# A list scheduler that ranks by what follows, six plans instead of one, and ScalarE as the engine that rounds the second batch's queries and keys

## The chip, the cores and the metric

The kernel runs as one program on one core of a Trainium2 chip. The core has five engines that each take their own instructions strictly in order: TensorE (PE: matrix products; PEld is its loading of weights), VectorE (DVE), ScalarE (ACT), GpSimd (POOL) and SyncE (SP, which here only issues transfers; 16 DMA engines carry them out). The metric is the device time of one execution in microseconds.

## The reference

Three layers follow each other, on 2 batches of 768 tokens.

- Attention, 8 heads of 64 columns. Six sign bits of `q @ proj` and `k @ proj` make a bucket number for each query and key; `mask = q_bucket == k_bucket`; `scores = where(mask, q @ k.T / 8, -1e9)`; `attn = softmax(scores)`; `out = attn @ v`.
- On the heads put side by side (768 x 512): `u = x + real(fft(fft(x, axis=1), axis=2))`, a normalisation of `u`'s rows, and `u + relu(un @ w_ch1) @ w_ch2` with an inner width of 2048.
- `h = gelu(x @ w_in)`, split into `u` and `v` of 512 columns; `v` is normalised and scaled by `g_ln`, mixed over the tokens by `w_sg` plus a bias, and `x + (u * v_s) @ w_out` is the result.

The weights come in 64-bit floats; all is held to float32 accuracy, so nearly every product is made of a high and a low half in 16 bits.

## The kernel before, in words

**Attention.** A head has six tiles of 128 queries, so there are 96 tiles, 48 in each batch. For a tile TensorE makes the scores `s` (L394), VectorE takes the row maximum (L404), ScalarE the exponential `e` (L406). Then `e` is cut into two 16-bit halves `eh` (L251 on ScalarE or L253 on GpSimd, and the remainder L258 on GpSimd), SyncE turns `eh` over by a transposing transfer (L445), and TensorE multiplies by the values (18 products per tile, L462 to L464). In batch 0 two tiles of six (`FLIP`) are turned over on TensorE instead (L430, L457, L460).

**Queries and keys.** Before its scores a head is prepared in `stacks`: `q1`, a rounded copy of the head's queries and keys (entry `hi` of `ENG`: VectorE L255 in batch 0, GpSimd L253 in batch 1, called by `copy`), `k2`, the rest (VectorE L265), and four moves of 64 partitions to the other half (`mv`; S stands for a transfer by SyncE, A for ScalarE, P for GpSimd; `ENG0` is for the very first head). Then ScalarE writes the one-hot bucket codes into `q1` and `k1` (L287, L289), out of a product `ct` (L360) of the sign bits (`bits`, L280, from `z`, L311). Heads whose number is in `FULL` skip this: their scores are one product in full float32 rather than two rounded ones.

**Weights.** A weight arrives as pieces `wide` of 64-bit words (L221); VectorE makes 32-bit floats of each in three steps (L226 to L228), ScalarE sums their squares (L230), one small product adds the sums over the partitions (`pb`, L139), and the two halves are written by ScalarE (L239) and VectorE (L241). `w1a` is made during batch 0's attention, the other halves of the two big weights (`w2a`, `w1b`, `w2b`) during batch 1's, the last layer's weights after it.

**Stages.** Attention of batch 0; then, at the same time, attention of batch 1, the Fourier step of batch 0 (`fft`; products y L549 and p L575) with its normalisation, and the first of the big layers for batch 0 (`ch`: c1 L667, its outputs halved by L675 and L676, and c2 L688); then the Fourier step and `ch` of batch 1; then the last layer (gi L764, sg L787, go L804).

**What sets the order.** The program is first recorded in one order. The class `Order` then plans anew: it takes every operation with a cost for each engine, walks through time, and on each engine starts the operation that is ready and stands first in the recorded order. Its transfer costs are guesses of the kernel's own. The plan's order is then fixed on each engine (`apply`): an engine whose next instruction waits stands still, even if a later one could run.

Of the kernel before, what the change touches and what calls it, by code (L numbers as in the profile page):

```python
# [21 lines left out]
P = 128  # L22
# [32 lines left out]
WB = (3, 2)  # L55
ENG = ({'oh': 'A', 'hi': 'D', 'mv': 'SSSS', 'cast': 'PPA', 'sub': 'P'}, {'oh': 'A', 'hi': 'P', 'mv': 'SSSS', 'cast': 'AAP', 'sub': 'P'})
GP = ''
FULL = (3, 11)
ZP = (False, False)
CP = (False, False)  # L60
ENG0 = {'hi': 'D', 'mv': 'AASA', 'oh': 'A'}
W_ATT0 = 1.5
# [868 lines left out]
class Node:  # L931
    def __init__(self, k, eng):
        self.k, self.eng = k, eng
        self.ins, self.acc, self.dep, self.succ, self.tiles = [], [], {}, [], []
        self.cost, self.size, self.turn, self.port = 0.0, 0, False, False


class Order:
# [5 lines left out]
    GAP = {"DVE": 0.19, "POOL": 0.13}  # L944
    LOOK, OVER = 12, 0.3
    LAP = {"PE": 0.0, "DVE": 0.075, "ACT": 0.1, "POOL": 0.045, "SP": 0.0}

# [34 lines left out]
    def cost(self, i, rd, wr):  # L982
# [32 lines left out]
    def read(self):  # L1015
# [3 lines left out]
        for i in self.tc.nc.cur_bb.bb.instructions:  # L1019
# [14 lines left out]
            n.cost += self.cost(i, rd, wr)  # L1034
            n.port = self.port(i, e, rd, wr)
            if e == "SP":
                n.turn = "Transpose" in type(i).__name__
                n.size = wr[0][2] * wr[0][5] * wr[0][7] if not wr[0][1] else (wr[0][2] - wr[0][1]) * wr[0][5] * wr[0][7]
# [52 lines left out]
    def choose(self, nodes, now, t, held):  # L1091
        n = nodes[heapq.heappop(now)]
        wait = held - t - 0.2
        if n.port and wait > 0.0 and now:
            for k in sorted(now)[:self.LOOK]:
                m = nodes[k]
                if not m.port and m.cost < wait + self.OVER:
                    now.remove(k)
                    heapq.heapify(now)
                    heapq.heappush(now, n.k)  # L1100
                    return m
        return n

    def plan(self):
# [10 lines left out]
        need = [len(n.dep) for n in nodes]  # L1115
        when, start = [0.0] * N, [0.0] * N
# [4 lines left out]
        wire, held = 0.0, [0.0, 0.0]  # L1121

        def room(n):
# [25 lines left out]
        for _ in range(N):  # L1149
            while True:  # L1150
                best = None
                for e in clock:
                    while later[e] and later[e][0][0] <= clock[e]:
                        heapq.heappush(now[e], heapq.heappop(later[e])[1])
# [5 lines left out]
                while later[e] and later[e][0][0] <= t:  # L1160
                    heapq.heappush(now[e], heapq.heappop(later[e])[1])
                n = self.choose(nodes, now[e], t, held[e == "DVE"] if e in ("DVE", "POOL") else 0.0)
                r = room(n)
                if r is None:
                    continue
                if r > t:
                    heapq.heappush(later[e], (r, n.k))
                    continue
                break
# [17 lines left out]
            start[n.k] = t  # L1187
            done = end + self.AFTER[e]
            for p in {self.home[x] for x in n.tiles}:
# [12 lines left out]
            for m in n.succ:  # L1202
# [6 lines left out]
                if not need[m.k]:  # L1209
                    push(m)  # L1210
        return order
# [100 lines left out]
```

## Time and profile before

| what | us |
|---|---|
| median of 3 runs | 706.52 |
| lowest and highest of them | 701.41, 707.3 |
| profiled execution, own time | 704.52 |
| its span, first to last instruction | 702.7 |

The profile is of one execution. The span is 1.8 us shorter than the execution's own time. A share says how much of the span an engine was busy; a wait is put down to the instruction that ended it; the granted clock is TensorE's, as a part of 2.4 GHz.

### The profile page before, as it was taken

The page shows a single profiled execution, that of the slowest core. Times are in us where ns is not written, and L with a number is a line of the kernel's source. Part 1 is how long each engine was busy: PE and PEld are TensorE (multiplying, and loading weights), DVE is VectorE, ACT ScalarE, POOL GpSimd, SP SyncE. Part 2 cuts the span into 40 slices and gives each one's busy share as a digit, 9 for nine tenths or more (in the row PEclk, how much of TensorE's full clock was granted, in tenths as well). Part 3 has the DMA queues.
Part 4 walks back from the last instruction along what each step waited for, and adds up shares of the span by engine and source line. Part 5 has one row for each costly group of instructions (what it writes and reads, how often), then busy time and mean ns, then how long its engine had stood idle before and what let it go on. Part 6 is the DMA issues. An engine that isn't in the chain of part 4 may idle for free.

```text
span 702.7 us, 12575 instructions
## 1 busy us (share of the span) xinstructions
PE 634.3 (90%) x4832; PEld 415.7 (59%) x4832; DVE 500.3 (71%) x1136; ACT 343.8 (49%) x533; POOL 237.0 (34%) x203
## 2 busy tenths in 40 slices
PE   3689998976787889899999999988999999999997
PEld 0577777844464666668687658645767444444443
DVE  6777756659799879798667299668663367776663
ACT  4778888965475765466562224214552044222010
POOL 1355656668367953255454032000000012111000
PEclk8799999987798999999999999999999999999999
DMA  8699999999998997869654014853100022112234
GB/s 324 180 173 164 187 231 187 207 231 278 226 198 177 202 206 197 181 149 216 131 93 137 1 31 76 255 138 102 61 1 1 1 46 45 25 24 40 64 90 120
DMA packets 184044, 94.79 MB, mean 135 GB/s; under 512 B 166512, under 2 KB 167280, under 8 KB 183472
## 3 DMA queue, kind: packets, MB, share of 16 engines
q1 hardware_dynamic: 183408, 93.85, 60.1%
q8 instruction: 38, 0.62, 0.4%
q10 hardware_dynamic: 576, 0.14, 0.1%
q14 instruction: 22, 0.18, 0.1%
HBM read 39.50 MB, written 3.15 MB: 61 GB/s over the span
## 4 chain that ended last, share of the span: by engine, by line
PE 58%; DVE 12%; DMA 12%; issue 6%; ACT 5%; POOL 5%; SPq 1%; ACTq 0%; POOLq 0%; DVEq 0%
PE c L688 13%; PE c L667 11%; PE gi L764 9%; PE sg L787 7%; DMA et<-eh 5%; PE go L804 4%; PE s L394 4%; POOL eh L258 3%; PE z L311 3%; DMA wide<-w 2%; DMA wide<-w_in 2%; DVE nm L404 2%; DVE w L228 2%; ACT e L406 1%; PE po L457 1%
## 5 line engine op out<-in xcount | busy, mean ns | idle before, releaser
L258 POOL TENSOR_TENSOR eh<-e,eh 128x768 f16<-128x768 f32 x80 | 141.0, 1765 | 95.3 <-ACT eh L251 90.7
L667 PE MATMUL c<-unT,w 128*128 128x256 f16 x1152 | 136.9, 279 | 7.9 <-DVE h L676 6.0
L667 PEld LDWEIGHTS <-w 128*128 128x128 f16 x1152 | 114.3, 100 | 28.2 <-issue 8.6
L688 PE MATMUL c<-w,h 128*128 128x512 f16 x576 | 130.2, 381 | 0.0
L394 PE MATMUL s<-k,q 128*128 128x384 f32 x384 | 101.3, 392 | 22.8 <-ACT k L289 15.7
L404 DVE TENSOR_REDUCE nm<-s 128x1 f32<-128x768 f32 x96 | 91.0, 951 | 36.4 <-PE s L394 36.2
L406 ACT ACTIVATE e<-s,nm 128x768 f32<-128x768 f32 x96 | 85.5, 896 | 41.8 <-DVE nm L404 26.5
L688 PEld LDWEIGHTS <-h 128*128 128x128 f16 x576 | 55.8, 99 | 63.6 <-issue 2.4
L394 PEld LDWEIGHTS s<-k,q 128*128 128x128 f32 x384 | 68.2, 201 | 31.2 <-ACT k L289 16.3
L780 POOL TENSOR_TENSOR vh<-gv,vh 128x512 f16<-128x512 f32 x12 | 13.9, 1157 | 197.3 <-ACT vh L779 197.3
L462 PE MATMUL pav<-V,et 128*128 128x65 f16 x480 | 54.7, 198 | 16.7 <-DMA et<-eh 12.1
L462 PEld LDWEIGHTS <-et 128*128 128x128 f16 x480 | 45.4, 101 | 28.6 <-DMA et<-eh 16.2
L463 PE MATMUL pav<-V,et 128*128 128x64 f16 x480 | 54.3, 196 | 0.0
L464 PE MATMUL pav<-V,et 128*128 128x65 f16 x480 | 54.1, 198 | 0.0
L675 ACT ACTIVATE h<-c 128x256 f16<-128x256 f32 x96 | 35.2, 378 | 34.6 <-PE c L667 34.3
L764 PE MATMUL gi<-in,xT 128*128 128x512 f16 x216 | 50.5, 379 | 0.0
L676 DVE SCALAR_TENSOR_TENSOR h<-c,h 128x256 f16<-128x256 f32 x96 | 38.3, 415 | 16.8 <-ACT h L675 16.8
L764 PEld LDWEIGHTS <-xT 128*128 128x128 f16 x288 | 28.2, 98 | 35.0 <-issue 1.1
L463 PEld LDWEIGHTS <-et 128*128 128x128 f16 x480 | 45.9, 100 | 2.3 <-issue 1.6
L464 PEld LDWEIGHTS <-et 128*128 128x128 f16 x480 | 46.0, 100 | 0.0
L251 ACT ACTIVATE eh<-e 128x768 f16<-128x768 f32 x48 | 40.2, 840 | 7.2 <-DMA et<-eh 6.6
L253 POOL TENSOR_SCALAR eh<-e 128x768 f16<-128x768 f32 x32 | 30.6, 956 | 34.3 <-ACT e L406 28.2
(221 smaller groups left out, 999.7 us busy)
## 6 DMA issues: line engine op xcount, KB each, us to landing
wide<-w SPq DMA_DIRECT2D x24, 512.0 KB, 4.5
x<-qk SPq DMA_DIRECT2D x16, 384.0 KB, 4.5
k<-q SPq DMA_DIRECT2D x26, 192.0 KB, 3.6
wide<-w SPq DMA_DIRECT2D x4, 1024.0 KB, 8.8
wide<-w_in SPq DMA_DIRECT2D x16, 256.0 KB, 3.1
vst<-v SPq DMA_DIRECT2D x8, 396.0 KB, 4.2
y<-ot SPq DMA_DIRECT2D x12, 256.0 KB, 2.3
q<-k SPq DMA_DIRECT2D x14, 192.0 KB, 3.7
```

What stands on the lines that cost most here:

```text
L251: self.nc.scalar.activation(out, src, AF.Copy, scale=scale)
L258: (self.nc.vector if eng == "D" else self.nc.gpsimd).tensor_tensor(out=out, in0=a, in1=b, op=ALU.subtract)
L394: nc.tensor.matmul(s[:, hf, 0:HS], q[:, qs], k[:, hf * HS:(hf + 1) * HS], start=n == 0, stop=n == len(pairs) - 1)
L404: nc.vector.tensor_reduce(nm, x["s"], axis=AX.XY, op=ALU.max, negate=True)
L406: nc.scalar.activation(e.rearrange("p (a c) -> p a c", a=2), x["s"], AF.Exp, bias=nm)
L462: nc.tensor.matmul(pv[:, qt, 0:65], et[:, kb, :], V[:, hl, kb, 64:129], start=kb == 0, stop=False)
L463: nc.tensor.matmul(pv[:, qt, 0:64], et[:, kb, :], V[:, hl, kb, 0:64], start=False, stop=False)
L464: nc.tensor.matmul(pv[:, qt, 0:65], et[:, NT + kb, :], V[:, hl, kb, 64:129], start=False, stop=kb == NT - 1)
L667: nc.tensor.matmul(ps[:, 0:step], w1[kc][:, a, fo], uT[:, 4 * u + kc, o * P:o * P + step], start=m == 0, stop=m == 11)
L688: nc.tensor.matmul(ps, hs[n, half, f][:, a, j * P:(j + 1) * P], wv[:, w, :], start=f + m == 0, stop=f == NF - 1 and m == 2)
L764: nc.tensor.matmul(ps, xT[:, 4 * a + kc, :], w_in[kc][:, w, half * DM:(half + 1) * DM], start=n == 0, stop=n == 11)
L787: nc.tensor.matmul(ps, w_sg[kt][:, w, t * P:(t + 1) * P], vh[b][:, kt, a, :], start=n == 0, stop=n == 17)
```

## The change

Three entries of the tables at the top change. In batch 1 the rounding of queries and keys (`hi`) moves from GpSimd to ScalarE. Head 11 leaves `FULL` and is prepared as the other heads are. Of the first head's four moves, the two that write `q2` go to GpSimd (they were one on ScalarE, one on SyncE), and the last, which writes `k2`, stays on ScalarE.

The planner changes in three ways. An operation that is ready is now taken by a rank, not by its place in the recorded order. `best` makes six plans: one with the recorded order as rank, and five whose rank mixes the start in the best plan so far with `tails`, the longest chain of work that follows an operation (over its data, and over the buffers it frees, `slots`); it keeps the plan that its own costs say ends first. And the costs themselves change: a transposing transfer goes at 192e3 bytes per us instead of 294e3, one inside the on-chip memory at 224e3, one from outside at 367e3 instead of 350e3, with other latencies; TensorE's operations pass through a helper (`warm`) that lets them run at full or half pace.

```diff
-ENG = (..., {'oh': 'A', 'hi': 'P', 'mv': 'SSSS', 'cast': 'AAP', 'sub': 'P'})
+ENG = (..., {'oh': 'A', 'hi': 'A', 'mv': 'SSSS', 'cast': 'AAP', 'sub': 'P'})
-FULL = (3, 11)
+FULL = (3,)
-ENG0 = {'hi': 'D', 'mv': 'AASA', 'oh': 'A'}
+ENG0 = {'hi': 'D', 'mv': 'APPA', 'oh': 'A'}
...
+    BLEND = (0.0, 0.25, 0.5, 0.75, 0.9)
...
+        if e == "ACT" and "DMA" in kind.upper():
+            return 0.1
...
     def choose(self, nodes, now, t, held):
-        n = nodes[heapq.heappop(now)]
+        n = nodes[heapq.heappop(now)[1]]
...
-                heapq.heappush(later[n.eng], (max(t, when[n.k]), n.k))
+                heapq.heappush(later[n.eng], (max(t, when[n.k]), self.rank[n.k], n.k))
...
             if e == "SP":
-                clock[e] = t + (1.44 + max(0.0, min(3.0, (wire - t - 2.8) * 0.8)) if n.turn else 0.5)
-                wire = max(t + (1.0 if n.turn else 1.3), wire) + n.size / (294e3 if n.turn else 350e3)
-                end = wire + (1.3 if n.turn else 0.75)
+                clock[e] = t + (1.44 + max(0.0, min(3.0, (wire - t - 3.2) * 0.8)) if n.turn else 0.5)
+                wire = max(t + (1.24 if n.turn else 1.8), wire) + n.size / ((196e3 if n.turn > 1 else 192e3) if n.turn else 224e3 if n.move else 367e3)
+                end = wire + (0.47 if n.turn else 0.69)
+            elif e == "PE":
+                end = clock[e] = self.warm(t, n.cost)
...
+    def tails(self):
+
+        tail = [0.0] * len(self.nodes)
+        for n in sorted(self.nodes, key=lambda n: (-n.start, -n.k)):
+            d = n.end - n.start
+            best = d
+            for m in n.succ:
+                if m.dep[n.k]:
+                    best = max(best, d + (0.0 if m.eng == n.eng else self.AFTER[n.eng]) + tail[m.k])
+            for m in n.follow:
+                best = max(best, d + self.AFTER[n.eng] + tail[m.k])
+            tail[n.k] = best
+        return tail
+
+    def best(self):
+        self.rank = list(range(len(self.nodes)))
+        self.slots()
+        t, order = self.plan()
+        found = t, order, [(n.start, n.end) for n in self.nodes]
+        begin = [n.start for n in self.nodes]
+        for f in self.BLEND:
+            tail = self.tails()
+            self.rank = [f * x - (1.0 - f) * y for x, y in zip(begin, tail)]
+            t, order = self.plan()
+            if t < found[0]:
+                found = t, order, [(n.start, n.end) for n in self.nodes]
+                begin = [n.start for n in self.nodes]
+        return found[1]
 
     def apply(self):
...
-        for ns in self.plan().values():
+        for ns in self.best().values():
```

The new plan reaches every engine. Two places follow, and one piece of TensorE's order. The rows of an order have no time in them; a number behind a name tells tiles of one name apart.

ScalarE at the start of the program, before: from the squares of the first values (`V`, L322) to the first exponential.

```order
L322 ACTIVATE V_183,vmx_184<-vst_175 128x12x64
L280 ACTIVATE bits0_73<-z_177,tiny_143 24x768
L334 ACTIVATE V_183<-vst_175,iv00_98 128x12x64
L230 ACTIVATE w1_0_157,wacc_226<-w1_1_158 128x1024
L322 ACTIVATE V_355,vmx_356<-vst_347 128x12x64
L230 ACTIVATE w1_0_157,wacc_226<-w1_2_159 128x1024
L251 ACTIVATE k2_200<-q1_197 64x768
L287 ACTIVATE q1_197<-ct_207,pops_61 64x768
L289 ACTIVATE k1_198<-ct_207,pops_61 64x768
L230 ACTIVATE w1_0_157,wacc_226<-w1_3_160 128x1024
L406 ACTIVATE e_224<-s_212,nm_222 128x768
```

The same place after the change, up to the second exponential.

```order
L251 ACTIVATE k1_198<-q1_197 64x768
L251 ACTIVATE k2_200<-q1_197 64x768
L280 ACTIVATE bits0_73<-z_177,tiny_143 24x768
L322 ACTIVATE V_183,vmx_184<-vst_175 128x12x64
L287 ACTIVATE q1_197<-ct_207,pops_61 64x768
L289 ACTIVATE k1_198<-ct_207,pops_61 64x768
L230 ACTIVATE w1_0_157,wacc_226<-w1_1_158 128x1024
L406 ACTIVATE e_224<-s_212,nm_222 128x768
L334 ACTIVATE V_183<-vst_175,iv00_98 128x12x64
L406 ACTIVATE e_242<-s_217,nm_240 128x768
```

Ahead of the one-hot codes (L287, L289) there stood two squares of weight pieces (L230), the values' first rounding (L334) and the squares of the next group's values; now only the first squares of values stand there.

ScalarE where batch 0's first c1 result is halved (L675), before and then after: L641 is the normalised row of batch 0, L406 and L251 are exponentials of batch 1 and their upper halves, L239 is the upper half of `w2a`.

```order
L406 ACTIVATE e_3150<-s_3069,nm_3148 128x768
L251 ACTIVATE eh_3229<-e_3150 128x768
L641 ACTIVATE hl_2978<-un_2977 128x512
L287 ACTIVATE q1_3020<-ct_3101,pops_61 64x768
L289 ACTIVATE k1_3021<-ct_3101,pops_61 64x768
L406 ACTIVATE e_3236<-s_3145,nm_3234 128x768
L641 ACTIVATE hl_2984<-un_2983 128x512
L675 ACTIVATE h1_3043<-c1_3030 128x256
```

```order
L406 ACTIVATE e_3553<-s_3467,nm_3551 128x768
L641 ACTIVATE hl_2988<-un_2987 128x512
L406 ACTIVATE e_3624<-s_3546,nm_3622 128x768
L239 ACTIVATE w1_4_161<-w2_0_2125,i_w2a_88 128x1024
L641 ACTIVATE hl_2994<-un_2993 128x512
L239 ACTIVATE w2_0_2125<-w2_1_2126,i_w2a_88 128x1024
L406 ACTIVATE e_3683<-s_3617,nm_3681 128x768
L251 ACTIVATE eh_3674<-e_3624 128x768
L675 ACTIVATE h1_3055<-c1_3042 128x256
```

More of batch 1's tiles, and two of the four halves of `w2a`, now stand ahead of the first c1. On TensorE 70 tiles have their scores and 50 have been multiplied by the values through a transposing transfer when the first c1 comes in the order before; after, 76 and 55.

TensorE, after the change, at the sum of the squares of `w_in` (`wm`, product pb) in the second `ch`; the rows around it are those of before but for the numbers of tiles.

```order
L688 MATMUL c2_6484<-w1_4_161,h1_6107 128x512
L139 MATMUL pb_6128<-wm_5701,ones_59 128x1
L667 LDWEIGHTS w1_0_157
L667 MATMUL c1_6134<-unT_5556,w1_0_157 128x256
L667 LDWEIGHTS w1_0_157
```

From the second Fourier step's end to this product 252 products c1 stand in both orders, and 126 products c2 before, 132 after. When that Fourier step begins, 552 c1 and 192 c2 are done in both. The last layer's products stand as before.

## Rows read from the trace of the kernel before

**Rows 1.** The page: busy time, share of the span and instructions of each engine.

```profile
PE 634.3 (90%) x4832; PEld 415.7 (59%) x4832; DVE 500.3 (71%) x1136; ACT 343.8 (49%) x533; POOL 237.0 (34%) x203
```

**Rows 2.** Busy time of each engine in five stretches; columns named in row one.

```profile
core 0: us, PE busy (x) PEld busy (x) DVE busy (x) ACT busy (x) POOL busy (x), PEclk, DMA share, GB/s
0.00:25.60 25.60, 9.01 (x20) 4.41 (x21) 15.96 (x28) 12.65 (x19) 2.72 (x18) 0.77 0.90 317
25.60:151.50 125.90, 112.61 (x1145) 92.33 (x1144) 85.65 (x131) 102.65 (x138) 78.99 (x64) 0.97 0.97 185
151.50:231.60 80.10, 58.48 (x521) 39.32 (x521) 70.76 (x132) 48.87 (x75) 53.26 (x45) 0.82 1.00 222
231.60:386.40 154.80, 148.97 (x1409) 109.87 (x1410) 122.42 (x206) 88.32 (x139) 76.52 (x54) 0.97 0.77 168
386.40:702.70 316.30, 305.21 (x1740) 169.81 (x1737) 205.54 (x642) 91.35 (x166) 25.46 (x24) 0.99 0.26 62
```

**Rows 3.** Timeline of ScalarE, 9 to 27 us: start, duration, line, form, idle before.

```profile
10.00 0.89 ACT L280 ACTIVATE bits<-z,tiny 24x768 f16<-24x768 f32 x1 [1.75 <-PE z L311]
11.41 0.94 ACT L334 ACTIVATE V<-vst,iv 128x768 f16<-128x768 f32 x1 [0.52 <-DVE iv L151]
15.82 1.06 ACT L230 ACTIVATE w<-w 128x1024 f32<-128x1024 f32 x1 [3.48 <-DVE w L228]
...
16.88 0.83 ACT L322 ACTIVATE V<-vst 128x768 f16<-128x768 f32 x1
...
20.18 0.84 ACT L251 ACTIVATE k<-q 64x768 fp32r<-64x768 f32 x1
...
21.96 0.90 ACT L289 ACTIVATE k<-ct,pops 64x768 fp32r<-64x768 f32 x1
...
25.59 0.90 ACT L406 ACTIVATE e<-s,nm 128x768 f32<-128x768 f32 x1 [1.56 <-DVE nm L404]
```

**Rows 4.** Timeline of TensorE where the first scores are made.

```profile
22.91 4.53 PE L394 MATMUL s<-k,q 128*128 128x384 f32 x13 [11.48 <-ACT k L289]
```

**Rows 5.** Waits of TensorE after 386 us: us in total, times, longest.

```profile
PE pb L139 <- issue: 3.5, 1, 3.5
PE c L667 <- DVE h L676: 2.9, 1, 2.9
```

**Rows 6.** Waits of GpSimd, the same columns.

```profile
POOL q L253 <- PE s L394: 7.2, 1, 7.2
```

**Rows 7.** Instructions of the tile x: ns min/median/max, first and last start.

```profile
L253 POOL TENSOR_SCALAR q<-x,qsc x7: 903/907/1987, 123.4 to 313.9; 128x768 fp32r<-128x768 f32 x7
```

**Rows 8.** Groups of instructions (with shapes): busy us, mean ns of one, idle before.

```profile
L404 DVE TENSOR_REDUCE nm<-s 128x1 f32<-128x768 f32 x96 | 91.0, 951 | 36.4 <-PE s L394 36.2
...
L227 DVE SCALAR_TENSOR_TENSOR w<-wide,w 128x512 int32<-128x512 int32 x16 | 15.1, 943 | 0.2
L265 DVE SCALAR_TENSOR_TENSOR k<-x,qsc,q 128x768 fp32r<-128x768 f32 x14 | 15.1, 1077 | 0.8 <-POOL q L253 0.6
L228 DVE SCALAR_TENSOR_TENSOR w<-wide,w 128x512 int32<-128x512 int32 x16 | 14.2, 887 | 0.2
L226 DVE TENSOR_SCALAR w<-wide 128x512 int32<-128x512 int32 x16 | 11.2, 707 | 7.9 <-DMA wide<-w 7.9
...
L241 DVE SCALAR_TENSOR_TENSOR w<-w,i_w2a,w 128x1024 f16<-128x1024 f32 x4 | 5.4, 1359 | 0.0
```

**Rows 9.** Timeline of TensorE: scores of a stacked head, of a FULL head.

```profile
59.61 0.94 PE L394 MATMUL s<-k,q 128*128 128x384 f32 x4
...
75.28 1.46 PE L394 MATMUL s<-k,q 128*128 128x384 f32 x4
```

**Rows 10.** Timeline of TensorE: first and last of the 18 products of one tile.

```profile
149.51 0.20 PE L462 MATMUL pav<-V,et 128*128 128x65 f16 x1 [1.71 <-DMA et<-eh]
...
150.03 0.20 PE L464 MATMUL pav<-V,et 128*128 128x65 f16 x1
```

**Rows 11.** Chain that ended last: start, us, what.

```profile
335.92 2.59 PE c L688 x12
```

More of the change, by code (lines that the diff above doesn't have):

```diff
@@ L934, in __init__ @@
         self.ins, self.acc, self.dep, self.succ, self.tiles = [], [], {}, [], []
-        self.cost, self.size, self.turn, self.port = 0.0, 0, False, False
+        self.cost, self.size, self.turn, self.port, self.move = 0.0, 0, 0, False, False
+        self.start, self.end, self.follow, self.far = 0.0, 0.0, [], False
 class Order:
@@ L945 @@
     LOOK, OVER = 12, 0.3
+    WINDOW = 3.413
+    BLEND = (0.0, 0.25, 0.5, 0.75, 0.9)
     LAP = {"PE": 0.0, "DVE": 0.075, "ACT": 0.1, "POOL": 0.045, "SP": 0.0}
@@ L1035, in read @@
             n.port = self.port(i, e, rd, wr)
+            n.far = e == "ACT" and "DMA" in type(i).__name__.upper()
             if e == "SP":
-                n.turn = "Transpose" in type(i).__name__
+                n.turn = int("Transpose" in type(i).__name__)
+                n.move = bool(rd and wr) and rd[0][0] in self.tiles and wr[0][0] in self.tiles
                 n.size = wr[0][2] * wr[0][5] * wr[0][7] if not wr[0][1] else (wr[0][2] - wr[0][1]) * wr[0][5] * wr[0][7]
@@ L1091, in choose, with warm @@
     def choose(self, nodes, now, t, held):
-        n = nodes[heapq.heappop(now)]
+        n = nodes[heapq.heappop(now)[1]]
         wait = held - t - 0.2
         if n.port and wait > 0.0 and now:
-            for k in sorted(now)[:self.LOOK]:
-                m = nodes[k]
+            for x in sorted(now)[:self.LOOK]:
+                m = nodes[x[1]]
                 if not m.port and m.cost < wait + self.OVER:
-                    now.remove(k)
+                    now.remove(x)
                     heapq.heapify(now)
-                    heapq.heappush(now, n.k)
+                    heapq.heappush(now, (self.rank[n.k], n.k))
                     return m
         return n
+    def warm(self, t, cost):
+        w = self.ham
+        while cost > 1e-9:
+            while w[0] + self.WINDOW <= t:
+                if not w[2] and w[1] < 0.48 * self.WINDOW:
+                    w[2] = 1
+                elif w[2] and w[1] >= 0.9 * self.WINDOW:
+                    w[2] = 0
+                w[0], w[1] = w[0] + self.WINDOW, 0.0
+            pace = 2.0 if w[2] else 1.0
+            d = min(cost * pace, w[0] + self.WINDOW - t)
+            t, cost, w[1] = t + d, cost - d / pace, w[1] + d
+        return t
     def plan(self):
@@ L1115, in plan @@
         need = [len(n.dep) for n in nodes]
-        when, start = [0.0] * N, [0.0] * N
+        when = [0.0] * N
         clock = dict.fromkeys(self.AFTER, 0.0)
@@ L1121, in plan @@
         wire, held = 0.0, [0.0, 0.0]
+        self.ham = [0.0, self.WINDOW, 0]
+        last = 0.0
         def room(n):
@@ L1143, in push, with ripe @@
             if t is not None:
-                heapq.heappush(later[n.eng], (max(t, when[n.k]), n.k))
+                heapq.heappush(later[n.eng], (max(t, when[n.k]), self.rank[n.k], n.k))
+        def ripe(e, t):
+            while later[e] and later[e][0][0] <= t:
+                heapq.heappush(now[e], heapq.heappop(later[e])[1:])
         for n in nodes:
@@ L1152, in plan @@
                 for e in clock:
-                    while later[e] and later[e][0][0] <= clock[e]:
-                        heapq.heappush(now[e], heapq.heappop(later[e])[1])
+                    ripe(e, clock[e])
                     t = clock[e] if now[e] else max(clock[e], later[e][0][0]) if later[e] else None
@@ L1159, in plan @@
                 clock[e] = t
-                while later[e] and later[e][0][0] <= t:
-                    heapq.heappush(now[e], heapq.heappop(later[e])[1])
+                ripe(e, t)
                 n = self.choose(nodes, now[e], t, held[e == "DVE"] if e in ("DVE", "POOL") else 0.0)
@@ L1166, in plan @@
                 if r > t:
-                    heapq.heappush(later[e], (r, n.k))
+                    heapq.heappush(later[e], (r, self.rank[n.k], n.k))
                     continue
@@ L1186, in plan @@
             order[e].append(n)
-            start[n.k] = t
-            done = end + self.AFTER[e]
+            n.start, n.end = t, end
+            last = max(last, end)
+            done = end + self.AFTER[e] + (2.5 if n.far else 0.0)
             for p in {self.home[x] for x in n.tiles}:
@@ L1210, in plan, with slots @@
                     push(m)
-        return order
+        return last, order
+    def slots(self):
+        use, first, line = {}, {}, {}
+        for n in self.nodes:
+            for t in n.tiles:
+                if t not in use:
+                    use[t], first[t] = [], n
+                    line.setdefault(self.over[t], []).append(t)
+                use[t].append(n)
+        for key, ts in line.items():
+            b = self.tiles[ts[0]].tag_meta.bufs or 1
+            for old, t in zip(ts, ts[b:]):
+                for n in use[old]:
+                    if n.k < first[t].k:
+                        n.follow.append(first[t])
+    def tails(self):
[24 more added lines that the diff above has]
+        return found[1]
     def apply(self):
         info = mybir.DependencyInfo(mybir.DependencyClass.NoSync, mybir.DependencyReason.DATA)
-        for ns in self.plan().values():
+        for ns in self.best().values():
             prev = None
```

2 lines of the change are left out of this document (1 added, 1 removed).

## The prediction, made before the changed kernel was run

> **What bounds the kernel now.** I read four views. First the page's engine totals [rows 1]: TensorE is busy 634.3 us of the span of 702.7, so at most 68 us can be had from its idle time, and whatever the change does must show there. Then the table of stretches [rows 2], cut where the program's stages change: the start, up to the first exponential (0 to 25.6 us); a second, attention of batch 0 (to 151.5); a third, from the first step of batch 0's Fourier transform to its first c1 product (to 231.6); a fourth, where c1 and c2 fill TensorE beside batch 1's attention (to 386.4, the start of the second Fourier step); a fifth, the rest. TensorE's idle time in them is 16.6, 13.3, 21.6, 5.8 and 11.1 us. The reader should see that the engine nearest its limit differs: in the second TensorE (112.6 of 125.9) with ScalarE behind it (102.7); in the third VectorE (70.8 of 80.1) with the transfers (share 1.00), while the granted clock is 0.82; in the fourth and fifth TensorE (149.0 of 154.8, 305.2 of 316.3). Then ScalarE's timeline of the start [rows 3] and the waits [rows 5, 6] for single places. The profiled execution took 704.52 us, 2.0 less than the median of 706.52; my sum is made against 704.5 and I add nothing for that difference.
>
> **The start.** The first scores begin at 22.91, and TensorE waits 11.48 us for the one-hot code of `k` (L289) before them [rows 4]. ScalarE was not short of time: its codes stood behind two squares of weight pieces (15.82 and the one after L322, 1.06 each, both waiting for VectorE) [rows 3]. In the new order they stand behind the bits and one square of values only. The bits start at 10.00 and take 0.89, the square 0.83 (some 0.2 for reading its sum), two codes 0.90 each [rows 3]: the scores begin at about 13.7. The first exponential came 25.59 - 22.91 = 2.7 us after them and would now come at 16.4. If VectorE is a step of a weight piece late with the first maximum (an estimate of 1.4 us, twice the 0.71 of a half-sized step [rows 8]), at 17.8. So 7.8 to 9.2 us earlier; I take **-8.6**. The two `q2` moves on GpSimd do not delay this: it has 2.7 us of work in the whole stretch [rows 2].
>
> **Batch 0's attention.** What was overtaken is not gone: two squares (2 x 1.06), the values' rounding (0.94) and the next squares (0.83) [rows 3], 3.9 us of ScalarE, now run among the exponentials. ScalarE has 23 us idle there and TensorE 13.3 [rows 2], so the price lies between 0 and 3.9; nearer to 0, because ScalarE is not the fuller engine: **+1.5**. VectorE's postponed pieces have 40 us of idle time there (125.9 - 85.7) and cost nothing; if that cover were gone, 1.4 us a step.
>
> **The Fourier step of batch 0.** Here the new order puts more ahead of the first c1. Counted in the two orders from the first `fe` (L527) to the first L676, VectorE has 5 more maxima (5 x 0.951), 2 steps of `w2a` (2 x 1.359), 2 remainders `k` (2 x 1.077) and one more piece (0.943 + 0.887 + 0.707) [rows 8]: 4.8 + 2.7 + 2.2 + 2.5 = 12.2 us. VectorE is idle 9.3 us of that stretch [rows 2]. If all of that were filled, the stretch grows by 12.2 - 9.3 = 2.9 us; if VectorE stays busy at its 88%, by 12.2 / 0.88 = 13.8. No row says which; I take the middle, **+8.4**. In it ScalarE's roundings hide: GpSimd had 7 of them of 0.907 us at the median [rows 7], ScalarE gets 8 (three of them here) of some 0.84, an estimate from its copy of as many columns [rows 3], and is busy 48.9 of 80.1 us [rows 2]. GpSimd's relief (6.3 us) is worth nothing by itself: it is busy 53.3 of 80.1.
>
> **Beside c1 and c2.** What was done early need not be done here. Ahead of the first c1 the new order has 76 score tiles instead of 70 and 55 value tiles instead of 50; at the second Fourier step both orders have done the same. Before, 26 score tiles were left, 2 of them of the FULL head 11 at 1.46 us and 24 at 0.94 [rows 9]: 25.5 us. Now 20 at 0.94: 18.8. A value tile's 18 products run from 149.51 to 150.03 [rows 10], some 0.55 us; five fewer are 2.7. Together -9.4 of TensorE's work in a stretch where it is 96% busy. Its 5.8 us of idle time may stay or go; I take half: **-9.4 - 2.9 = -12.3** (between -9.4 and -15.2).
>
> **The rest.** The order is nearly the old one, and the wait of 3.5 us before the product pb of `w_in`, like the 2.9 us before a c1 [rows 5], comes from a chain of transfers and conversions of `w_in` that stands as before. Six more c2 products are put ahead of pb, 0.216 us each (12 in 2.59 [rows 11]): **-1.3**. Both waits gone would be -6.4; the first doubled, because four pieces of `w_sg` now precede `w_in`, +3.5.
>
> **Sum.** -8.6 + 1.5 + 8.4 - 12.3 - 1.3 = -12.3: 704.5 - 12.3 = **692 us**. All favourable ends: -9.2 + 0 + 2.9 - 15.2 - 6.4 = -27.9, 677. All unfavourable ends: -7.8 + 3.9 + 13.8 - 9.4 + 3.5 = +4.0, 708.
>
> **Rivals.**
>
> *More than that (680 us).* The new transfer costs make the plan fit the chip, so that fewer instructions stand in an engine's way. For it: TensorE idles 13.3 us in batch 0's attention, and some of it is spent before value products whose transfer has not landed (1.71 us ahead of the product at 149.51 [rows 10]). If half of that goes (-6.6) and VectorE fills its gaps in the Fourier step (+2.9 instead of +8.4): 692.2 - 6.6 - 5.5 = 680. Against: the distance of value products behind scores is much the same in both orders.
>
> *Nothing (704.5 us).* TensorE is not what limits the fourth stretch, which then keeps its 154.8 us: 704.5 - 7.1 + 8.4 - 1.3 = 704.5; what the start gains is spent in the Fourier step. For it: a pipelined engine's busy share can hide gaps, and its weight loads are busy only 109.9 of 154.8 us [rows 2]. Against: 12 c2 products in 2.59 us [rows 11] are 0.216 each for 512 columns, and 512 columns at 2.4 GHz are 0.213. The Trainium skill, Perfetto Trace Analysis, section Identifying the Most-Contended Engine, says the matmul share is no measure of how near TensorE is to its limit and that the weight loads' share is; by it TensorE would be 71% used there and this rival the forecast. The trace does not bear that out where c2 runs, and I keep it as a rival.
>
> *Slower (721 us).* ScalarE's queue is in order, and the roundings now stand in it ahead of exponentials. On GpSimd one of them waited 7.2 us, for the last scores that read the buffer it overwrites [rows 6]; there only remainders stood behind it. On ScalarE everything that feeds VectorE, GpSimd and the transposing transfers stands behind it. Where such a wait falls in batch 0's attention or the Fourier step (four roundings), it adds its length: 4 x 7.2 = 28.8 on top of 692. Two such waits use up the forecast's gain; in the fourth stretch ScalarE has 66 us idle and absorbs them. Against: only one of seven waited so before, and the plan knows of the buffer.
>
> *The change does not do what it says.* The rows of both orders show that it does; what they cannot show is whether a long chain, rather than the new costs, moved a given row.
>
> **How the numbers follow.** Forecast 0.48, more 0.17, nothing 0.18, slower 0.12, anything else 0.05. The time is the forecast's, 692. The range takes in the forecast's two ends, 677 and 708, with 680 and 704.5 inside, and is drawn to 710 because runs of this kernel differ by a few us; it leaves out the slower case and a little below. About 1% is what a measurement of this kernel can tell from no change: 699.5 and 713.6 around 706.5. Faster by more: three quarters of the forecast's cases (0.36), all of the larger gain (0.17), something of the rest: 0.60. Within 1%: the other quarter, the case of nothing: 0.27. Slower: 0.13.
>
> **What would show it.** In the changed kernel's profile: the first exponential at 16.4 to 17.8 us; the first `fe` some 7 us earlier than 151.5; from there to the first c1 83 to 94 us instead of 80.1, with VectorE over 88% busy; from the first c1 to the second Fourier step 140 to 145 us instead of 154.8; no wait of ScalarE's L251 for scores above a microsecond or two; a wait before pb of 2 to 4 us. The prediction is wrong if the fourth stretch does not shrink, or if the Fourier step grows by more than its gain.

## The result, and the profile after

The change ran in 696.12 us (median of 4 runs, 692.43 to 698.07) against 706.89 us of the kernel before on the same chip: ratio 0.9866, 95% interval 0.9821 to 0.9911. The profiled execution took 692.43 us, its span 690.6. The median lies 4 us above the forecast of 692 and inside its range of 677 to 710. The profiled execution is the fastest of the four, so what its profile shows is a little more than the change gains as a rule. In it the stretches add up to what was forecast; what makes the kernel faster is not what the forecast took it to be, which only the experiments showed.

The windows of the changed kernel, with the columns of [rows 2] and cut at the same events (first exponential, first `fe`, first c1, second Fourier step, end):

```profile
0.00:15.50 15.50, 7.50 (x24) 3.45 (x24) 11.37 (x24) 7.63 (x10) 4.71 (x18) 1.00 0.86 324
15.50:144.30 128.80, 113.48 (x1146) 93.17 (x1147) 93.54 (x139) 110.50 (x151) 79.35 (x65) 0.97 1.01 205
144.30:232.50 88.20, 64.00 (x632) 48.31 (x629) 80.60 (x141) 59.84 (x86) 61.96 (x49) 0.79 1.10 240
232.50:379.40 146.90, 139.02 (x1295) 102.53 (x1295) 113.31 (x196) 79.41 (x130) 60.92 (x43) 0.98 0.71 156
379.40:690.60 311.20, 303.73 (x1741) 169.40 (x1739) 204.38 (x643) 90.43 (x166) 25.33 (x24) 1.00 0.27 63
```

Set against [rows 2], the five lengths changed by -10.1, +2.9, +8.1, -7.9 and -5.1 us: -12.1. Forecast were -8.6, +1.5, +8.4, -12.3 and -1.3: -12.3. In the fourth stretch TensorE's busy time fell by 9.95 us and its idle time rose from 5.8 to 7.9.

ScalarE's timeline at the start, the place of [rows 3], and TensorE's first scores, the place of [rows 4]:

```profile
9.30 0.89 ACT L280 ACTIVATE bits<-z,tiny 24x768 f16<-24x768 f32 x1
...
11.04 0.89 ACT L287 ACTIVATE q<-ct,pops 64x768 fp32r<-64x768 f32 x1
11.95 0.90 ACT L289 ACTIVATE k<-ct,pops 64x768 fp32r<-64x768 f32 x1
...
15.54 0.90 ACT L406 ACTIVATE e<-s,nm 128x768 f32<-128x768 f32 x1 [1.52 <-DVE nm L404]
16.34 0.93 ACT L334 ACTIVATE V<-vst,iv 128x768 f16<-128x768 f32 x1
```

```profile
12.89 1.33 PE L394 MATMUL s<-k,q 128*128 128x384 f32 x6 [1.44 <-ACT k L289]
```

Only one square of values (L322) stands between the bits and the codes, the values' rounding (L334) comes after the first exponential, and TensorE waits 1.44 us for the code of `k` instead of 11.48.

TensorE's waits in the last stretch, which answer to [rows 5], are total us, times and longest:

```profile
PE c L688 <- DVE xu L692: 1.7, 1, 1.7
PE pb L139 <- issue: 1.1, 1, 1.1
```

The c1 that waited 2.9 us no longer does, pb waits 1.1 us instead of 3.5, and a c2 waits 1.7 us that did not wait before. The roundings on ScalarE (instructions of L251, ns min/median/max) answer to [rows 7]:

```profile
L251 ACT ACTIVATE q<-x,qsc x8: 919/925/936, 108.8 to 297.6; 128x768 fp32r<-128x768 f32 x8
```

0.925 us each, where the forecast estimated 0.84 and GpSimd took 0.907. In ScalarE's waits between 15.5 and 379.4 us two rows have L251, and neither is such a rounding or a wait for scores:

```profile
ACT eh L251 <- DMA et<-eh: 2.5, 1, 2.5
ACT ef L251 <- PE tp L430: 2.1, 4, 0.7
```

**Where the third stretch grew.** The stretch from the first `fe` to the first c1 has a natural cut: the first normalised row that ScalarE rounds for c1 (`hl`, L641). Windows of the kernel before, up to it and behind it, and then of the change:

```profile
151.50:221.60 70.10, 52.23 (x453) 35.38 (x454) 61.03 (x112) 41.45 (x65) 44.46 (x38) 0.79 1.00 223
221.60:231.60 10.00, 6.24 (x69) 3.94 (x67) 9.73 (x21) 7.41 (x12) 8.80 (x7) 1.00 0.99 215
```

```profile
144.30:213.70 69.40, 52.58 (x519) 38.85 (x516) 62.80 (x108) 45.34 (x67) 47.91 (x38) 0.82 1.10 247
213.70:232.50 18.80, 11.42 (x115) 9.46 (x113) 17.80 (x34) 14.51 (x19) 14.04 (x11) 0.68 1.08 214
```

Up to the first row the length is nearly the same (70.1, 69.4). The growth lies behind it, 10.0 to 18.8 us, where more work of batch 1 now stands ahead of the first c1 (115 products on TensorE instead of 69) and VectorE is busy 17.8 us instead of 9.7. TensorE's timeline there, with the wait before a group in brackets:

```profile
216.89 0.97 PE L394 MATMUL s<-k,q 128*128 128x384 f32 x4 [0.67 <-ACT e L406]
...
221.08 1.65 PE L394 MATMUL s<-k,q 128*128 128x384 f32 x4 [3.22 <-ACT k L289]
...
231.03 1.65 PE L394 MATMUL s<-k,q 128*128 128x384 f32 x4 [3.25 <-ACT e L406]
232.48 0.86 PE L667 MATMUL c<-unT,w 128*128 128x256 f16 x3
```

One wait for a code is 3.22 us long, one for an exponential 3.25, and c1 stands right behind the tile that had the second. After each the same four products take 1.65 us instead of 0.97: the granted clock is 0.68 on the mean of this stretch, a mixture of the two levels (1.2 and 2.4 GHz).

### The profile page after: what moved, and what is told of

It reads as the page before. It is cut to its first block, busy times and chain, and to the rows that moved or that the text cites. A ratio compares the mean times of both kernels' runs of the same rounds, so it can differ in the third digit from the quotient of the medians.

```text
span 690.6 us, 12566 instructions
## 1 busy us (share of the span) xinstructions
PE 627.7 (91%) x4832; PEld 416.9 (60%) x4832; DVE 503.2 (73%) x1137; ACT 347.8 (50%) x540; POOL 232.3 (34%) x197
## 4 chain that ended last, share of the span: by engine, by line
PE 44%; DVE 10%; DMA 5%; ACT 2%; POOL 1%; issue 1%; DVEq 0%; POOLq 0%; ACTq 0%
PE c L667 10%; PE c L688 9%; PE gi L764 9%; PE sg L787 7%; PE go L804 5%; DMA wide<-w_in 3%; DMA wide<-w 1%; PE y L549 1%; PE s L394 1%; DVE xu L692 1%; DVE w L241 1%; DVE h L676 1%; DVE nm L404 1%; DVE in L227 1%; DVE w L227 1%
## 5 line engine op out<-in xcount | busy, mean ns | idle before, releaser
L258 POOL TENSOR_TENSOR eh<-e,eh 128x768 f16<-128x768 f32 x80 | 138.5, 1735 | 103.1 <-ACT eh L251 100.8
L688 PE MATMUL c<-w,h 128*128 128x512 f16 x576 | 131.7, 379 | 1.7 <-DVE xu L692 1.7
L406 ACT ACTIVATE e<-s,nm 128x768 f32<-128x768 f32 x96 | 85.2, 896 | 40.2 <-DVE nm L404 28.1
L394 PEld LDWEIGHTS s<-k,q 128*128 128x128 f32 x384 | 69.4, 205 | 41.0 <-ACT e L406 21.7
L688 PEld LDWEIGHTS <-h 128*128 128x128 f16 x576 | 55.5, 98 | 60.9 <-issue 2.6
L675 ACT ACTIVATE h<-c 128x256 f16<-128x256 f32 x96 | 35.0, 377 | 60.4 <-PE c L667 59.9
L462 PEld LDWEIGHTS <-et 128*128 128x128 f16 x480 | 46.6, 103 | 16.4 <-issue 10.6
L463 PEld LDWEIGHTS <-et 128*128 128x128 f16 x480 | 46.6, 101 | 1.9 <-issue 0.7
L464 PEld LDWEIGHTS <-et 128*128 128x128 f16 x480 | 46.5, 101 | 0.0
L253 POOL TENSOR_SCALAR eh<-e 128x768 f16<-128x768 f32 x32 | 32.7, 1022 | 32.2 <-ACT e L406 25.6
L251 ACT ACTIVATE eh<-e 128x768 f16<-128x768 f32 x48 | 40.3, 839 | 3.0 <-DMA et<-eh 2.5
```

Source lines behind the costliest of these rows:

```text
L258: (self.nc.vector if eng == "D" else self.nc.gpsimd).tensor_tensor(out=out, in0=a, in1=b, op=ALU.subtract)
L394: nc.tensor.matmul(s[:, hf, 0:HS], q[:, qs], k[:, hf * HS:(hf + 1) * HS], start=n == 0, stop=n == len(pairs) - 1)
L406: nc.scalar.activation(e.rearrange("p (a c) -> p a c", a=2), x["s"], AF.Exp, bias=nm)
L462: nc.tensor.matmul(pv[:, qt, 0:65], et[:, kb, :], V[:, hl, kb, 64:129], start=kb == 0, stop=False)
L463: nc.tensor.matmul(pv[:, qt, 0:64], et[:, kb, :], V[:, hl, kb, 0:64], start=False, stop=False)
L464: nc.tensor.matmul(pv[:, qt, 0:65], et[:, NT + kb, :], V[:, hl, kb, 64:129], start=False, stop=kb == NT - 1)
```

## The experiments

The forecast's theory: the gain comes from the order at the start and from work that the ranks move ahead of the first c1, at the price of VectorE's load in the Fourier step. One rival: it comes from the transfer costs, whatever the ranks and entries do. Another: from the engine that rounds. Each ratio is to the kernel before on the same chip, with its 95% interval. The six times are those of one profiled execution: the starts of the first exponential, first `fe`, first `hl`, first c1 and second Fourier step, and the end. Kernels are compared by their ratios; the times serve to compare stretches.

| kernel | ratio | interval | first e | fe | hl | c1 | 2nd Fourier | end |
|---|---|---|---|---|---|---|---|---|
| before | 1 | | 25.6 | 151.5 | 221.6 | 231.6 | 386.3 | 702.7 |
| the change | 0.9866 | 0.9821-0.9911 | 15.5 | 144.3 | 213.7 | 232.5 | 379.4 | 690.6 |
| tables_only | 0.9958 | 0.9930-0.9985 | 17.4 | 154.3 | 220.2 | 234.4 | 385.6 | 702.6 |
| old_costs | 0.9969 | 0.9938-0.9999 | 17.2 | 154.5 | 220.0 | 234.1 | 386.0 | 703.2 |
| planner_only | 0.9761 | 0.9713-0.9810 | 24.7 | 150.1 | 208.9 | 223.6 | 369.1 | 685.9 |
| one_plan | 0.9796 | 0.9746-0.9845 | 15.8 | 145.5 | 206.4 | 225.1 | 372.1 | 689.5 |
| transfer_costs | 0.9819 | 0.9781-0.9858 | 24.4 | 150.7 | 206.8 | 221.6 | 374.4 | 689.3 |
| two_paces | 1.0076 | 1.0036-1.0116 | 26.3 | 157.5 | 229.0 | 245.9 | 401.4 | 712.5 |
| late_rank | 0.9721 | 0.9681-0.9760 | 25.2 | 149.6 | 209.0 | 223.9 | 369.2 | 682.1 |
| late_rank_entries | 0.9783 | 0.9758-0.9807 | 15.8 | 145.2 | 205.9 | 224.7 | 370.8 | 686.7 |
| late_start | 0.9973 | 0.9947-1.0000 | 24.5 | 151.7 | 222.5 | 241.3 | 388.3 | 700.6 |
| same_plan_gpsimd | 0.9849 | 0.9795-0.9902 | 16.2 | 145.1 | 216.8 | 234.0 | 379.1 | 690.2 |
| less_vector | 0.9876 | 0.9830-0.9921 | 16.3 | 144.0 | 216.2 | 234.7 | 381.8 | 693.8 |
| more_vector | 0.9941 | 0.9911-0.9970 | 15.2 | 145.0 | 220.3 | 239.3 | 386.5 | 698.7 |

The first four take the change apart into entries, costs and ranks.

**tables_only**: the kernel before with the three new entries.

```diff
-ENG = (..., {'oh': 'A', 'hi': 'P', ...})
+ENG = (..., {'oh': 'A', 'hi': 'A', ...})
-FULL = (3, 11)
+FULL = (3,)
-ENG0 = {'hi': 'D', 'mv': 'AASA', 'oh': 'A'}
+ENG0 = {'hi': 'D', 'mv': 'APPA', 'oh': 'A'}
```

> The three table entries with the planner of before. Theory 1, the order the new planner finds carries the gain: within 4 us of before, some 3 us off for head 11's scores (6 tiles of 0.5 us) at the most, and a first exponential that is not earlier than 20 us. Rival, the entries carry it (the first head's moves on GpSimd, the roundings on ScalarE): 8 to 12 us faster than before, with a first exponential at 15 to 17 us.

**planner_only**: the change with the three old entries, that is, the new planner alone.

```diff
-ENG = (..., {'oh': 'A', 'hi': 'A', ...})
+ENG = (..., {'oh': 'A', 'hi': 'P', ...})
-FULL = (3,)
+FULL = (3, 11)
-ENG0 = {'hi': 'D', 'mv': 'APPA', 'oh': 'A'}
+ENG0 = {'hi': 'D', 'mv': 'AASA', 'oh': 'A'}
```

> The new planner with the three old table entries. Theory 1: 7 to 12 us faster than before, first exponential at 16 to 18 us. Rival, the entries: 0 to 3 us faster than before.

**one_plan**: the change without its five ranked plans.

```diff
-    BLEND = (0.0, 0.25, 0.5, 0.75, 0.9)
+    BLEND = ()
```

> The change without its five ranked plans: new entries, new costs, the recorded order as rank. If ranking by what follows makes the gain: 700 us or more, at most 5 us faster than before. If the truer costs make it: 692 to 698, like the change.

**old_costs**: the change with the old transfer costs, those of the four transfers that ScalarE issues among them, and TensorE at one pace, ranking kept.

```diff
...
-                wire = max(t + (1.24 if n.turn else 1.8), wire) + n.size / (...)
-                end = wire + (0.47 if n.turn else 0.69)
+                wire = max(t + (1.0 if n.turn else 1.3), wire) + n.size / (294e3 if n.turn else 350e3)
+                end = wire + (1.3 if n.turn else 0.75)
...
-                end = clock[e] = self.warm(t, n.cost)
+                end = clock[e] = t + n.cost
...
```

> The change with the old costs of transfers and TensorE at one pace, ranking kept. If ranking makes the gain: 692 to 698, like the change. If the costs make it: 702 us or more.

The entries alone are worth 0.4% (0.9958), the planner with the old entries 2.4% (0.9761): more than the whole change, with intervals apart. The early first exponential comes with the entries (17.4 us in tables_only) and not with the planner (24.7 in planner_only); which of the three brings it was not tested. In planner_only the recorded order wins among the six plans, so its order owes nothing to a rank: it is the new costs alone. In old_costs no ranked plan wins either, and its order is that of tables_only; the two ratios show how far one order differs from itself (0.9958, 0.9969). Where the recorded order is kept with the new entries (one_plan, 0.9796), the kernel is faster than where a rank wins (the change, 0.9866), but the intervals overlap by a quarter of a per cent. The planner's own sums are no guide at that scale: by them the plan that won in the change ends at 666.3 us and the recorded order at 667.2. Windows of one_plan up to the first `hl` and behind it:

```profile
145.50:206.40 60.90, 44.07 (x403) 30.28 (x401) 53.71 (x103) 39.02 (x60) 39.82 (x33) 0.78 1.02 240
206.40:225.10 18.70, 11.77 (x140) 8.84 (x137) 18.67 (x32) 12.07 (x16) 15.36 (x11) 0.86 1.04 215
```

So what the ranks cost lies ahead of the first row, 69.4 us in the change against 60.9, with VectorE busy 62.8 us against 53.7. The 18.8 us behind it are not theirs: one_plan needs 18.7.

In tables_only the first exponential also comes 8 us early, yet the first `fe` 2.8 us late. Its window of batch 0's attention:

```profile
17.40:154.30 136.90, 119.21 (x1166) 97.14 (x1165) 95.13 (x138) 109.51 (x149) 80.24 (x62) 0.95 0.94 189
```

136.9 us where [rows 2] have 125.9: the early start is spent before the stretch ends. This speaks against the forecast's theory and for the costs. The next runs ask what the start, the engine and VectorE are worth inside the change's own plan.

**late_start**: ten copies of 0.84 us on ScalarE ahead of the bits, of which the plan knows nothing.

```diff
+            for _ in range(10 if n + hl == 0 else 0):
+                self.copy("A", q1[64:128], x[64:128], SCALE)
...
```

> The change's own plan, with ten needless copies of 0.84 us on ScalarE ahead of the sign bits, unseen by the planner: the first exponential moves from 15.5 to 23.9 us. If the early start is what the change gains in batch 0's attention, the first fe comes 6 to 8.4 us later than at 144.3 and the kernel is 5 to 8 us slower than the change, near 701. If that stretch ends when something else lets it, the first fe moves by less than 3 us and the kernel by less than 3.

**same_plan_gpsimd**: the change's plan, but the eight roundings run on GpSimd, put into its queue by their planned start.

```diff
-ENG = (..., {'oh': 'A', 'hi': 'A', ...})
+ENG = (..., {'oh': 'A', 'hi': 'P', ...})
...
+                n.eng, n.real, n.port = "ACT", "POOL", False
...
```

> The change's own plan, but the eight roundings of batch 1 run on GpSimd at the moments that the plan gave them on ScalarE. The prediction's step (the roundings hide on ScalarE): within 2 us of the change. Rival, that entry costs what the old entries with the new planner are ahead: 3 to 7 us faster than the change.

**less_vector**: the second step of the eight pieces of `w2a` on 16 columns; the kernel leaves out the signs of the other columns.

```diff
+                few = slice(0, 16 if bank else m)
-                nc.vector.scalar_tensor_tensor(out=t, in0=hi, ..., in1=t, ...)
+                nc.vector.scalar_tensor_tensor(out=t[:, few], in0=hi[:, few], ..., in1=t[:, few], ...)
...
```

> The change's own plan; the second of the three conversion steps of the eight pieces of w2a runs on 16 columns instead of 512 (the signs of the other columns of w2a are left out), some 8 x 0.54 = 4.3 us less of VectorE between the first fe and the first c1. If VectorE sets that stretch (88.2 us), it shrinks by 3 to 4.3 us and the kernel by 2 to 4. If the chain of the Fourier step or the transfers set it: less than 1 us.

**more_vector**: the third step of those pieces three times, the plan unchanged.

```diff
+                for _ in range(3 if bank else 1):
                     nc.vector.scalar_tensor_tensor(out=to, in0=lo, ...)
...
```

> The change's own plan; the third conversion step of the eight pieces of w2a is run three times, 16 x 0.68 = 10.9 us more of VectorE in the same stretch, unseen by the planner. If VectorE sets it: 8 to 11 us longer, and the kernel 6 to 10 us slower than the change. If not: its idle 7.6 us take most of it, 0 to 4 us longer.

The engine that rounds is worth nothing that the runs can tell: with the roundings on GpSimd the ratio is 0.9849, within the change's interval. A first exponential 9 us later costs 7.4 us at the first `fe`, 8.8 at the first c1, and 7.5 of the whole by the ratios (0.9973): in a plan that is fixed, an early start does carry through. VectorE gives an answer that is not symmetric. 14 more instructions up to `hl`, 9.7 us, cost 5.9 us there (75.3 against 69.4), between the two outcomes expected; taking 3.6 us away gave nothing (72.2). The same plan with VectorE's work as it was takes 70.8 in late_start and 71.7 in same_plan_gpsimd, so some 2 us of such a difference tell nothing. Groups of VectorE's instructions between `fe` and `hl` (busy us, mean ns of one) say why, first of the change, then of less_vector, then of more_vector; the line numbers of the last two are one higher:

```profile
L227 DVE SCALAR_TENSOR_TENSOR wt<-wide,wt 128x512 int32<-128x512 int32 x7 | 4.8, 680 | 0.0
...
L531 DVE SCALAR_TENSOR_TENSOR ee<-fe,ix,ee 128x257 f16<-128x257 f32 x3 | 3.8, 1279 | 0.0
...
L598 DVE TENSOR_TENSOR xu<-xu,qdu 128x255 f32<-128x255 f32 x3 | 1.7, 559 | 0.0
L597 DVE TENSOR_TENSOR xu<-xu,qdu 128x257 f32<-128x257 f32 x3 | 1.7, 553 | 0.0
```

```profile
L532 DVE SCALAR_TENSOR_TENSOR ee<-fe,ix,ee 128x257 f16<-128x257 f32 x3 | 4.4, 1456 | 0.0
...
L599 DVE TENSOR_TENSOR xu<-xu,qdu 128x255 f32<-128x255 f32 x3 | 3.1, 1036 | 0.0
...
L598 DVE TENSOR_TENSOR xu<-xu,qdu 128x257 f32<-128x257 f32 x3 | 2.7, 887 | 0.0
...
L228 DVE SCALAR_TENSOR_TENSOR wt<-wide,wt 128x16 int32<-128x16 int32 x7 | 1.2, 165 | 0.0
```

```profile
L229 DVE SCALAR_TENSOR_TENSOR w<-wide,wt 128x512 int32<-128x512 int32 x21 | 14.4, 684 | 0.6
...
L532 DVE SCALAR_TENSOR_TENSOR ee<-fe,ix,ee 128x257 f16<-128x257 f32 x3 | 2.3, 775 | 0.0
...
L598 DVE TENSOR_TENSOR xu<-xu,qdu 128x257 f32<-128x257 f32 x3 | 1.3, 431 | 0.0
```

The same three instructions take 3.8, 4.4 or 2.3 us (`ee`), 1.7 or 2.7 (`xu` over 257 columns). What less_vector saves on the weights (3.6 us) returns as 0.6 + 1.4 + 1.0 on these. A place of the change shows the mechanism, VectorE's timeline and then GpSimd's:

```profile
164.24 0.68 DVE L527 TENSOR_TENSOR fe<-xu 128x512 f32<-128x512 f32 x1
164.85 1.49 DVE L531 SCALAR_TENSOR_TENSOR ee<-fe,ix,ee 128x257 f16<-128x257 f32 x1
```

```profile
164.39 1.67 POOL L528 TENSOR_TENSOR fo<-xu 128x512 f32<-128x512 f32 x1 [1.68 <-DVE oo L540]
```

`ee`, 0.47 us at its shortest, here ends at 166.34, 0.28 us after GpSimd's `fo` (166.06). The same holds for the first `xu` over 257 columns in less_vector, which ends 0.28 us after a GpSimd remainder:

```profile
193.65 1.10 DVE L598 TENSOR_TENSOR xu<-xu,qdu 128x257 f32<-128x257 f32 x1
```

```profile
192.82 1.65 POOL L259 TENSOR_TENSOR eh<-e,eh 128x768 f16<-128x768 f32 x1
```

The Trainium skill, SBUF — State Buffer, section Who interferes with whom, says that a VectorE instruction with two inputs in that memory contends with a GpSimd instruction that reads it, and that the ports which the two share are an exclusive lock; these places agree, with 1.0 us lost in the first.

The last runs take the planner apart, and use what it shows.

**transfer_costs**: planner_only with TensorE at one pace. As the recorded order wins, this is the kernel before with the new transfer costs.

```diff
-                end = clock[e] = self.warm(t, n.cost)
+                end = clock[e] = t + n.cost
```

> The old entries and the new transfer costs, TensorE at one pace; the recorded order as rank (it wins among the six plans with these entries). If the transfer costs make the gain of the new planner with old entries (0.976 of before): 685 to 692. If the two paces do: 700 or more.

**two_paces**: planner_only with the old transfer costs; only the four transfers that ScalarE issues keep the new one.

```diff
...
-                wire = max(t + (1.24 if n.turn else 1.8), wire) + n.size / (...)
-                end = wire + (0.47 if n.turn else 0.69)
+                wire = max(t + (1.0 if n.turn else 1.3), wire) + n.size / (294e3 if n.turn else 350e3)
+                end = wire + (1.3 if n.turn else 0.75)
```

> The old entries, the old transfer costs, TensorE at two paces. If the transfer costs make the gain: 699 or more. If the two paces do: 685 to 692.

**late_rank**: planner_only, but the recorded order ranks up to batch 1's big layers, and behind them a ranked plan is taken even where the planner's own costs put the recorded order first.

```diff
...
+            late = [n.k for n in self.nodes if n.k >= self.late]
+            self.rank = list(range(len(self.nodes)))
+            for r, k in zip(late, sorted(late, key=lambda k: key[k])):
+                self.rank[k] = r
...
```

> The old entries with the new costs; the recorded order as rank up to batch 1's second big layers, and one of the ranked plans after them, whatever the planner thinks of its end. If ranking is worth something where w_in and the second ch run side by side (5 us there in the change), 3 to 6 us below the old entries with the new planner, some 683. If that gain was the entries' or chance: 686 to 690.

**late_rank_entries**: late_rank with the change's three entries.

```diff
-ENG = (..., {'oh': 'A', 'hi': 'P', ...})
+ENG = (..., {'oh': 'A', 'hi': 'A', ...})
-FULL = (3, 11)
+FULL = (3,)
-ENG0 = {'hi': 'D', 'mv': 'AASA', 'oh': 'A'}
+ENG0 = {'hi': 'D', 'mv': 'APPA', 'oh': 'A'}
```

> late_rank with the change's three entries instead of the old ones (nothing else), so the first exponential comes at 15.5 to 16 us instead of 25.2. If the early start carries through a plan made with the new transfer costs, the second Fourier step of batch 1 begins about 8 us earlier than in late_rank and the ratio to the kernel before is 0.958 to 0.964. If it is lost again, as between the change's entries with one plan (0.9796) and the old entries with one plan (0.9761), the first fe comes 4 to 5 us earlier, the first c1 no earlier than the 223.9 us of late_rank, and the ratio is 0.970 to 0.978.

The transfer costs alone give 0.9819: that rival is borne out. The order is again the recorded one. It gains most in the Fourier step of batch 0: up to `hl` it needs 56.1 us instead of 70.1, with VectorE busy 51.0 of them instead of 61.0, and behind `hl` it gives back 4.8:

```profile
150.70:206.80 56.10, 45.35 (x446) 31.24 (x445) 51.04 (x104) 37.92 (x59) 42.02 (x37) 0.88 1.07 240
206.80:221.60 14.80, 8.18 (x74) 4.51 (x73) 14.77 (x27) 8.67 (x13) 12.57 (x10) 1.00 1.13 241
```

VectorE's longest waits up to `hl`, of the kernel before and then of transfer_costs:

```profile
DVE nm L404 <- PE s L394: 2.9, 3, 2.0
DVE wt L226 <- DMA wide<-w: 1.9, 1, 1.9
DVE yc L556 <- ACT yc L555: 1.8, 2, 1.7
```

```profile
DVE ys L556 <- ACT ys L555: 1.4, 1, 1.4
DVE yc L556 <- ACT yc L555: 0.9, 2, 0.6
DVE oeh L537 <- ACT oeh L536: 0.8, 1, 0.8
DVE nm L404 <- PE s L394: 0.6, 1, 0.6
```

The wait of a weight step for its piece (1.9 us) is gone, as it should be in a plan that knows when a transfer lands. Of the 14.0 us saved up to `hl`, 10.0 are VectorE's busy time (eight instructions fewer, others less stretched) and 4.0 its idle time; 5.0 us of VectorE's work come back behind `hl`, so over the whole stretch to the first c1 9.2 us are saved. How much of it each cost brings is open. With the new entries the same costs pay elsewhere: from tables_only to one_plan, 13.1 us apart at the end, the attention of batch 0 gets 7.2 us shorter and the stretch from there to the first c1 0.5.

Two paces on top of that (planner_only against transfer_costs) bring 0.9761 for 0.9819, with intervals that overlap. two_paces by itself is not that half alone: with the old transfer costs a ranked plan won, and it is the one kernel whose interval lies above 1. Its times go from 703.03 to 714.26 us, and its stretches are not compared.

Ranks pay in one place, the last stretch, from the second Fourier step to the end. By the table it takes 316.8 us in planner_only and 312.9 in late_rank; it takes 314.9 to 317.4 us in the kernels with the recorded order, and 311.1 to 312.3 in those where a rank orders the whole program. At 683.79 us (median) late_rank beats the kernel before and the change (its interval overlaps planner_only's, 0.9761). With the entries this is lost again (0.9783): at the end 4.6 us, of which 0.8 are there at the first c1 and 3.0 come in the last stretch, where its ranked plan needs 315.9 us. The windows up to the first c1, of late_rank and then of late_rank_entries:

```profile
25.20:149.60 124.40, 113.82 (x1153) 92.85 (x1153) 86.99 (x133) 106.62 (x142) 81.69 (x65) 0.99 0.94 191
149.60:223.90 74.30, 54.36 (x540) 36.54 (x538) 65.57 (x130) 49.83 (x75) 55.19 (x47) 0.91 1.06 240
```

```profile
15.80:145.20 129.40, 116.22 (x1154) 94.33 (x1154) 93.59 (x137) 109.91 (x149) 79.47 (x62) 0.98 0.98 203
145.20:224.70 79.50, 57.09 (x540) 40.08 (x537) 72.42 (x133) 51.13 (x75) 54.44 (x44) 0.77 1.02 234
```

9.4 us earlier at the first exponential, 5.0 us longer in attention, 5.2 longer to the first c1: nothing is left. One reason fits: VectorE work that the old order did during the long start (15.8 against 11.4 us) is done later, where VectorE is busy 13.5 us longer. That difference is more than the 4.4 us put off, and no run shows that it is the cause. In all kernels the transfers are near full up to the first c1 (mean share 0.96 to 1.03 from the program's start). No run took transfers away, so whether they too hold that time is open.

## Why the prediction was right, and where it was not

The sum came out (-12.1 against -12.3), and that is in part luck: the five terms were off by -1.5, +1.4, -0.3, +4.4 and -3.8 us, which add up to 0.2. Three of the signs named in advance were missed: the first exponential came before 16.4 us, the stretch beside c1 and c2 took 146.9 us and not 140 to 145, and pb waited 1.1 us and not 2 to 4.

**The start** (forecast -8.6, measured -10.1). The reading of ScalarE's queue was right; the bits came 0.7 us earlier than assumed, and no step of a weight delayed the first maximum. That the new planner's order brings it was wrong: it comes with the entries (tables_only). That this term is a gain of the kernel holds in part: late_start bears it out inside this plan, tables_only and late_rank_entries show that a plan with the same entries and other costs or ranks spends all of it by the first c1.

**Batch 0's attention** (+1.5, measured +2.9) lies within its bounds of 0 and 3.9, with ScalarE busy 7.9 us longer.

**The Fourier step** (+8.4, measured +8.1). Up to the first c1 VectorE's busy time grew by 9.8 us (70.8 to 80.6), where 12.2 were counted, and its idle time took 1.7 of them: the step held roughly, and the middle between 2.9 and 13.8 was a lucky choice, since no row told where to stand. Where the growth falls was not foreseen. The first normalised row came after the same 70 us, because two effects cancel there: ranks made that part 8.5 us longer than the recorded order with the same costs and entries (69.4 against 60.9), and costs and entries had made it shorter (70.1 to 60.9). The growth stands behind that row, where score tiles with waits of 3.22 and 3.25 us and a clock of 0.68 delay c1. That VectorE sets the stretch is likely but not shown: more_vector shows that its load can cost as much (5.9 us for 9.7), less_vector that relief does not come back, since instructions that GpSimd holds up have no fixed duration to count with.

**Beside c1 and c2** (-12.3, measured -7.9). TensorE's work fell by 9.95 us (forecast 9.4), so the count of tiles was right. Half of its idle time was to go as well; instead it grew by 2.1. The stretch behaves as one that TensorE sets: its work went, and most of the time with it. This ends the rival "nothing". The Trainium skill (Perfetto Trace Analysis, Identifying the Most-Contended Engine) names the share of weight loads, beside the use of peak FLOPs, as the measure of how near TensorE is to its limit. In this stretch that share (109.9 of 154.8 us before, 102.5 of 146.9 after) would have misled, and the share of matmuls did not; the use of peak FLOPs was not worked out.

**The rest** (-1.3, measured -5.1). The bound of -6.4, both waits gone, was nearly reached: 3.5 to 1.1 and 2.9 to none, with a new one of 1.7. That the waits come from a chain of `w_in` "that stands as before" failed; planner_only and late_rank keep waits of 3.5 and 3.2 us before pb, so it takes ranks over the whole program to move it.

**The rivals.** "Slower" fell: no rounding waited for scores. "More" had the right cause, new transfer costs that make the plan fit, at 0.17, and the sum gave that cause no term of its own. The changed kernel could not tell the two apart, because in it the winning rank gives back, up to `hl`, 8.5 us of what the costs bring (69.4 against 60.9 in one_plan).

## What to carry to other kernels

When one edit changes a planner's costs, its ranking and its inputs, run each alone before any is believed: here the costs alone gave 1.8%, costs with two paces 2.4%, the inputs 0.4%, and the ranking seems to have lost where it was let loose on the whole program (the intervals overlap) and gained in its last part. Time won at the start can be lost again in the next stages, as in three of the four plans here that have it: look at the later stretches before counting it. A busy time counted from durations is no fixed load where two engines exclude each other: test it in both directions.

## What the runs showed of the hardware

One form of VectorE instruction (`xu`, 257 columns) had a mean of 0.431 us in more_vector, 0.553 in the change and 0.887 in less_vector. It goes with what GpSimd did at the time: the long ones (0.79 us in the change, 1.10 and 1.07 in less_vector) each end 0.28 to 0.29 us after a GpSimd remainder that ran beside them, and those that met none took 0.39 to 0.42. Added VectorE work shortened other instructions in this way: 9.7 us of additions raised its busy time up to `hl` by 5.7 (62.8 to 68.5).
